# A loop on TensorE for the score matmuls of a decode attention kernel: register-addressed operands behind an opening matmul of zeros

## The chip, the cores and the metric

The kernel runs on one core of a Trainium2 chip. Its metric is device time in microseconds (us); in a profiled run it is 1.8 us longer than the span from the first to the last instruction. In this kernel TensorE does the matrix products, DVE (VectorE) the elementwise work and the reductions. In the traces TensorE's register and branch instructions are recorded apart from its matmuls; what runs the first is called its sequencer here, what runs the second the array. SBUF is the memory that the loads of this kernel fill, PSUM the one to which its matmuls write their sums, in banks. Each run below was taken beside runs of the kernel before on the same chip.

## The reference, cut to what matters

A residual stream `x` of one token (640 values) passes four attention layers in turn, A, B, A, B, each with its own key and value caches of 32 heads x 8192 positions x 192 values in bf16.

```python
q = (x @ wq).reshape(B, Sq, H, Dh)...                       # 1 token, 32 heads, 192
scores = jnp.einsum("bhqd,bhkd->bhqk", q, k_cache) * (Dh ** -0.5)
p = _softmax(scores, axis=-1)
o = jnp.einsum("bhqk,bhkd->bhqd", p, v_cache)
return o... @ wo
...
x = x + _A_ref(_layernorm(x), A_k_cache, A_v_cache, A_wq, A_wo)   # then B, A, B
```

Each cache element is used once in a layer, so nearly all the work is to bring 848 MB into the core and to touch it once.

## The kernel before

It works on pairs of heads. A pair's keys and values are 6144 KB each and go into eight slots of SBUF. A pair has two units `u`, one for each half of the positions. For a unit, DVE multiplies the keys by the query in four chunks of 48 of the 192 values, and TensorE adds the products up: 24 matmuls with the identity as the stationary operand sum 192 values down to eight, in one PSUM bank. A DVE reduction adds the last eight. The first matmul of a unit has `start=True`, the others `start=False`: the kernel relies on the first to overwrite what the bank held, and on the others to add to it. This is called opening the bank.

```python
def products(p, u):
    ...
    for c in range(4):                                       # DVE, four chunks
        d0 = c * QD
        e = DV.op(lambda v, d0=d0: v.tensor_tensor(
            k3[:, :, d0:d0 + QD], kin[:, :, d0:d0 + QD],
            q_sb[qi][:, d0:d0 + QD].unsqueeze(1).broadcast_to([P, JU, QD]), ALU.mult))
        chunks.append(e)
    S = SP_[u]
    PE.wait(last["S"][u], ev_const)
    for c in range(4):                                       # TensorE, six matmuls a chunk
        PE.wait(chunks[c])
        for r in range(QD // R):
            d0 = c * QD + r * R
            fin = c == 3 and r == QD // R - 1
            e = PE.op(lambda t, d0=d0, fin=fin: (
                t.matmul(S[:, :], lhsT=ident[:], rhs=k3[:, :, d0:d0 + R], start=True, stop=fin) if d0 == 0 else
                matmul_held(t, S[:, :], ident[:], k3[:, :, d0:d0 + R], False, fin)), signal=fin, bank=Su[u])
    freed[nt] = ev_S[p, u] = e                               # the key slot is free again

def softmax(p):
    ...
    for u in range(2):                                       # the reduction that waits for S
        ev_s = last["S"][u] = DV.op(lambda v, u=u: v.tensor_reduce(s[:, ...], SP_[u][:]..., AX.X, ALU.add), ev_S[p, u], ...)
```

`matmul_held` reuses the weights that are loaded: the trace of before has 128 weight loads for the 3072 score matmuls. After the softmax come the value matmuls and a gather, then the next pair's products. Loads are issued from SyncE as soon as the slot is free:

```python
def ahead():
    while issued[0] < len(plan):
        m = plan[issued[0]]
        if any(b not in freed for b in before[m]):
            return
        issued[0] += 1
        landed[m] = transfer(m)
```

Of the kernel before, what the change touches and what calls it, by code (L numbers as in the profile page):

```python
# [11 lines left out]
class Queue:  # L12
# [18 lines left out]
    def op(self, fn, *events, sem=None, inc=1, signal=True, bank=()):  # L31
# [11 lines left out]
            d[self] = (sem, self.counts[id(sem)])  # L43
        return sem, self.counts[id(sem)]

    def emit(self, eng):
        for it in self.items:
            if len(it) == 2:
                eng.wait_ge(*it)
            else:  # L50
                ins = it[0](eng)
                if it[1] is not None:
                    ins.then_inc(it[1], it[2])


def matmul_held(t, out, lhsT, rhs, start, stop, size=128, column=0):

    return t.add_instruction(mybir.InstMatmult(  # L58
        name=t.bass.get_next_instruction_name(), engine=mybir.EngineType.PE,
        ins=[t.lower_ap(rhs), t.lower_ap(lhsT, for_matmul_weights=True)], outs=[t.lower_ap(out)],  # L60
        start_tensor_calc=start, stop_tensor_calc=stop, tile_size=(128, size), tile_position=(0, column), ldweights=False))


PAIRS_W = 5
# [4 lines left out]
def build(nc, A_x, A_k, A_v, A_wq, A_wo, B_x, B_k, B_v, B_wq, B_wo, out):  # L69
    _, H, SK, DH = A_k.shape  # L70
    D = A_x.shape[-1]
    P = 128
# [6 lines left out]
    QD = DH // 4  # L79
    R = 512 // JU  # L80
# [17 lines left out]
    with ExitStack() as ctx:  # L98
        def sb(name, shape, dt):
            return ctx.enter_context(nc.sbuf_tensor(name, shape, dt))  # L100
# [4 lines left out]
        def sem(name):  # L105
            return ctx.enter_context(nc.semaphore(name))

        ident = sb("ident", [P, P], BF16)
# [38 lines left out]
        zero = sb("zero", [P, 33], BF16)  # L147
# [12 lines left out]
        Su = [(use["S0"],), (use["S1"],)]  # L160
# [6 lines left out]
        PE = Queue(sem("pPE"))  # L167
# [7 lines left out]
        e = PO.op(lambda g: g.memset(ident[:], 0.0))  # L175
# [6 lines left out]
        e = PO.op(lambda g: g.memset(mask, 0.0))  # L182
        for t in range(G):
            e = PO.op(lambda g, t=t: g.affine_select(
                out=mask, in_=mask, compare_op=ALU.not_equal, fill=1.0,
                base=-32 * t, pattern=[[-1, 2], [-2, VK]], channel_multiplier=1), e)
# [13 lines left out]
        def first_load(kind, l, p):  # L200

            n = (kind, pair(l, p))
            if l >= 2 and n in KEPT[l - 2]:
                return (l - 2, ORDER[l - 2]["pairs"].index(n[1]))
            return (l, p)

        def stays(kind, l, p):
            return l < 2 and (kind, pair(l, p)) in KEPT[l]
# [17 lines left out]
        for l in range(NL):  # L226
# [8 lines left out]
            for p in range(NPAIR):  # L235
# [17 lines left out]
                if p < NPAIR - 2:  # L253
                    if first_load("v", l, p) == (l, p):
                        plan += [("v", l, p, u) for u in range(2)]
                        if l == 2 and p == 1:
                            i = plan.index(("k", l, 1, 0))
# [135 lines left out]
        def need(n):  # L393

            while n not in landed:
# [3 lines that stand above are left out]
            return landed[n]  # L399
# [22 lines left out]
        def busy(n):  # L422

            PE.wait(ev_const, last["S"][0])
            for i in range(n):
                PE.op(lambda t, i=i: (
                    t.matmul(SP_[0][:, :], lhsT=ident[:], rhs=ident[:].unsqueeze(1).broadcast_to([P, 4, P]), start=True, stop=True)
                    if i == 0 else
                    matmul_held(t, SP_[0][:, :], ident[:], ident[:].unsqueeze(1).broadcast_to([P, 4, P]), True, True)),
                    signal=False, bank=Su[0])  # L430
# [14 lines left out]
        def layer(l, ev_z, ev_true):  # L445
# [7 lines left out]
            if l == 2:  # L453
                busy(2)
            e = DV.op(lambda v: v.scalar_tensor_tensor(out=nv[:], in0=mv[:, 0:1], scalar=mv[:, 0:1], in1=mv[:, 1:2],
                                                       op0=ALU.mult, op1=ALU.subtract))
            e = DV.op(lambda v: v.tensor_scalar(vs[:], nv[:], -float(DH), float(DH) * EPS, ALU.mult, ALU.add), e, last["rs"])
# [6 lines left out]
            if l < 2:  # L464
                e = need(("wq", l, 0))
# [4 lines left out]
            else:  # L470
                e = ev_first[l - 2]
                q_first = wq0[l - 2]
            PE.wait(e)
            for c in range(DC):
                for h in range(2):
                    e = PE.op(lambda t, c=c, h=h: t.matmul(
                        QM[64 * h:64 * h + 64, 0:DH], lhsT=xb[:, c:c + 1].broadcast_to([P, 64]),
                        rhs=q_first[:, c, h * DH:(h + 1) * DH], start=(c == 0), stop=(c == DC - 1)),
                        signal=(c == DC - 1 and h == 1), bank=QMu)
# [8 lines left out]
            def q_rows(g, r0=0, r1=None):  # L488

                n = ("wq", l, g)  # L490
                c0, k = Q_PARTS[g]
                t3 = wq_rows(l, g)[:, :, ORDER[l]["q1"] * PD if l < 2 else 0:]
                PE.wait(need(("wq", l, 0)) if l < 2 else need(n), ev_xb, last["O"], last["YB"], ev_first.get(l))
                r1 = k if r1 is None else r1
                for c in range(r0, r1):
                    for b in range(4):
                        w = min(512, QR - b * 512)
                        for r in range(3):
                            fin = c0 + c == DC - 1
                            o, x, y = (OY[32 * r:32 * r + 1, b * 512:b * 512 + w], xb[:, c0 + c:c0 + c + 1],  # L500
                                       t3[:, c, r * QR + b * 512:r * QR + b * 512 + w])
                            e = PE.op(lambda t, b=b, c=c, r=r, o=o, x=x, y=y, fin=fin: (
                                t.matmul(o, lhsT=x, rhs=y, start=c0 + c == 0, stop=fin) if b == 0 else
                                matmul_held(t, o, x, y, c0 + c == 0, fin, 32, 32 * r)),
                                signal=(c == r1 - 1 and b == 3 and r == 2), bank=OYu)
                freed.setdefault(n, e)
                if c0 + k == DC:
                    last["xb"] = e
                    last["rows"] = AC.op(
                        lambda a: a.activation(rows[0:65, :], OY[0:65, 0:QR], ACT.Copy, scale=rs[0:65, 0:1]),  # L510
                        e, ev_rs, last["qbc"], bank=OYu)
# [73 lines left out]
            def products(p, u):  # L585
                nk = ("k",) + first_load("k", l, p) + (u,)
                nt = ("t", l, p, u) if stays("k", l, p) else nk
                kin = slot[place[nk]].rearrange("p (j d) -> p j d", d=DH)
                k3 = slot[place[nt]].rearrange("p (j d) -> p j d", d=DH)
                qi = (l * NPAIR + p) % 2  # L590
                DV.wait(need(nk), need(nt), ev_q[p])
                chunks = []
                for c in range(4):
# [5 lines that stand above are left out]
                last["q"][qi] = chunks[-1]  # L599
                S = SP_[u]  # L600
                PE.wait(last["S"][u], ev_const)
                for c in range(4):
                    PE.wait(chunks[c])
                    for r in range(QD // R):
                        d0 = c * QD + r * R
                        fin = c == 3 and r == QD // R - 1
                        e = PE.op(lambda t, d0=d0, fin=fin: (
                            t.matmul(S[:, :], lhsT=ident[:], rhs=k3[:, :, d0:d0 + R], start=True, stop=fin) if d0 == 0 else  # L608
                            matmul_held(t, S[:, :], ident[:], k3[:, :, d0:d0 + R], False, fin)), signal=fin, bank=Su[u])
                freed[nt] = ev_S[p, u] = e  # L610

            def softmax(p):
# [107 lines left out]
            for n in [n for n in steps if n[1] == l]:  # L720
                if n[0] == "m":
                    products(*n[2:])
                elif n[0] == "s":
                    softmax(n[2])
# [37 lines left out]
            e = DV.op(lambda v: v.tensor_tensor(x_true[:], x_true[:], YB[:, 0:DC], ALU.add), ev_y, ev_true, bank=YBu)  # L762
# [5 lines left out]
        e = SP.op(lambda s: s.dma_start(out[0, 0].rearrange("(h n) -> h n", h=2), ev_z[0:33:32, :]), *ev_true, sem=semOUT, inc=16)  # L768
# [54 lines left out]
```

## Time and profile before

The first three runs had a median of 1985.24 us (1982.8 to 1987.34).

| What | Before | How to read it |
|---|---|---|
| Data queue's share of the 16 DMA engines | 99.6% | the resource that is hardly ever idle |
| TensorE, DVE busy | 65%, 61% | not free time: they run one after the other inside a pair |
| DVE's wait for keys | 133.3 + 97.2 us | 3.6 us in each of 64 pairs, what compute has to spare |
| DVE's reduction waits for S | 68.0 us | 1.06 us a pair, where a slower score stage shows first |

Its lines stand in the prediction below.

### The profile page before, as it was taken

The page shows a single profiled execution, that of the slowest core. Times are in us where ns is not written, and L with a number is a line of the kernel's source. Part 1 is how long each engine was busy: PE and PEld are TensorE (multiplying, and loading weights), DVE is VectorE, ACT ScalarE, POOL GpSimd, SP SyncE. Part 2 cuts the span into 40 slices and gives each one's busy share as a digit, 9 for nine tenths or more (in the row PEclk, how much of TensorE's full clock was granted, in tenths as well). Part 3 has the DMA queues.
Part 4 walks back from the last instruction along what each step waited for, and adds up shares of the span by engine and source line. Part 5 has one row for each costly group of instructions (what it writes and reads, how often), then busy time and mean ns, then how long its engine had stood idle before and what let it go on. Part 6 is the DMA issues. An engine that isn't in the chain of part 4 may idle for free.

```text
span 1980.6 us, 13926 instructions
## 1 busy us (share of the span) xinstructions
PE 1282.8 (65%) x8335; PEld 148.6 (8%) x3249; DVE 1201.2 (61%) x1377; ACT 139.6 (7%) x462; POOL 4.5 (0%) x23
## 2 busy tenths in 40 slices
PE   3567476566466666666785675666676766667658
PEld 0001001000100100100020010010002001001001
DVE  3566466467166656566745565665764765665756
ACT  0000000000000000000010000000000100000000
POOL 0000000000000000000000000000000000000000
PEclk9787777778687777777887777877886877777778
DMA  9999999999999999999999999999999999999998
GB/s 413 437 432 430 430 430 432 436 430 428 435 431 431 430 435 433 428 433 433 427 408 432 427 430 431 430 430 431 431 431 428 436 429 434 432 432 431 431 434 364
DMA packets 26786, 849.25 MB, mean 429 GB/s; under 512 B 3042, under 2 KB 3044, under 8 KB 3812
## 3 DMA queue, kind: packets, MB, share of 16 engines
q1 hardware_dynamic: 26580, 848.38, 99.6%
q8 instruction: 45, 0.74, 0.2%
q14 instruction: 17, 0.14, 0.0%
q10 hardware_dynamic: 144, 0.00, 0.0%
HBM read 848.36 MB, written 0.00 MB: 428 GB/s over the span
## 4 chain that ended last, share of the span: by engine, by line
DMA 67%; PE 17%; DVE 15%; ACT 1%; issue 0%; SPq 0%
DMA pool<-in_B_k_cache_dram 27%; DMA pool<-in_A_v_cache_dram 22%; DMA pool<-in_A_k_cache_dram 13%; DVE pool L595 13%; PE S L58 7%; DMA pool<-in_B_v_cache_dram 6%; PE OY L58 5%; PE OY L674 3%; DVE acc L693 1%; ACT p_sb L632 1%; DVE s_sb L617 1%; PE OY L535 1%; PE S L608 0%; DVE m_bf L619 0%; PE QM L622 0%
## 5 line engine op out<-in xcount | busy, mean ns | idle before, releaser
L595 DVE TENSOR_TENSOR pool<-pool,q_sb 128x3072 bf16<-128x3072 bf16 x512 | 860.8, 1751 | 231.9 <-DMA pool<-in_B_k_cache_dram 133.3
L58 PE MATMUL S<-pool,ident 128*128 128x512 bf16 x2944 | 788.6, 425 | 20.4 <-DVE pool L595 18.8
L704 PE MATMUL TB<-acc,small 128*1 128x192 f32 x240 | 82.7, 495 | 212.0 <-DVE acc L693 212.0
L58 PE MATMUL OY<-pool,p_sb 128*16 128x512 bf16 x1920 | 198.8, 490 | 0.0
L608 PE MATMUL S<-pool,ident 128*128 128x512 bf16 x128 | 62.4, 488 | 207.7 <-DVE pool L595 207.6
L692 DVE TENSOR_SCALAR acc<-OY,small 128x192 f32<-128x192 f32 x64 | 26.7, 418 | 277.9 <-PE OY L58 248.0
L674 PE MATMUL OY<-pool,p_sb 128*16 128x512 bf16 (+1 forms) x1216 | 145.9, 488 | 64.3 <-DMA pool<-in_A_v_cache_dram 59.7
L693 DVE SCALAR_TENSOR_TENSOR acc<-OY,small,acc 128x192 f32<-128x192 f32 x424 | 177.0, 418 | 14.9
L617 DVE TENSOR_REDUCE s_sb<-S 128x64 f32<-128x512 f32 x128 | 87.8, 686 | 68.0 <-PE S L58 68.0
L524 ACT ACTIVATE q_sb<-QM 128x192 bf16<-128x192 f32 x60 | 19.8, 330 | 952.4 <-PE QM L518 952.4
L715 ACT ACTIVATE rows<-TB,small 1x192 bf16<-1x192 f32 x120 | 43.1, 405 | 587.7 <-PE TB L704 587.7
L688 DVE RECIPROCAL small<-TB 1x2 f32<-1x2 f32 x64 | 11.2, 175 | 94.7 <-PE TB L647 75.3
L632 ACT ACTIVATE p_sb<-s_sb,small 64x128 bf16<-64x128 f32 x128 | 55.7, 435 | 160.9 <-DVE small L626 160.1
L608 PEld LDWEIGHTS S<-pool,ident 128*128 128x128 bf16 x128 | 12.9, 101 | 682.9 <-DVE pool L595 619.9
L647 PE MATMUL TB<-small,ones 128*1 128x2 f32 x120 | 11.4, 165 | 74.1 <-ACT p_sb L632 74.1
L674 PEld LDWEIGHTS OY<-pool,p_sb 128*16 128x16 bf16 (+1 forms) x1216 | 38.9, 105 | 207.4 <-issue 133.1
L622 PE MATMUL QM<-ident,m_bf 128*64 128x64 bf16 x128 | 14.1, 217 | 54.4 <-DVE m_bf L619 53.8
L704 PEld LDWEIGHTS TB<-acc,small 128*1 128x1 f32 x240 | 19.8, 102 | 311.2 <-DVE acc L693 284.0
L535 PE MATMUL OY<-oT,pool 128*128 128x1 bf16 x825 | 34.9, 178 | 2.5 <-ACT oT L580 2.5
L626 DVE TENSOR_REDUCE small<-QM 128x1 f32<-128x64 f32 x64 | 14.3, 224 | 35.2 <-PE QM L622 35.2
L535 PEld LDWEIGHTS OY<-oT,pool 128*128 128x128 bf16 x825 | 33.9, 131 | 4.5 <-ACT oT L580 3.2
L518 PEld LDWEIGHTS QM<-rows,one_b 1*64 1x64 bf16 x120 | 6.2, 100 | 347.1 <-issue 341.2
(75 smaller groups left out, 205.0 us busy)
## 6 DMA issues: line engine op xcount, KB each, us to landing
pool<-in_B_k_cache_dram SPq DMA_DIRECT2D x28, 6144.0 KB, 38.1
pool<-in_B_v_cache_dram SPq DMA_DIRECT2D x28, 6144.0 KB, 33.5
pool<-in_A_v_cache_dram SPq DMA_DIRECT2D x27, 6144.0 KB, 27.6
pool<-in_A_k_cache_dram SPq DMA_DIRECT2D x34, 3072.0 KB, 19.9
pool<-in_A_k_cache_dram SPq DMA_DIRECT2D x14, 6144.0 KB, 36.5
pool<-in_A_v_cache_dram SPq DMA_DIRECT2D x10, 3072.0 KB, 14.3
pool<-in_B_k_cache_dram SPq DMA_DIRECT2D x8, 3072.0 KB, 22.4
pool<-in_A_wo_dram SPq DMA_DIRECT2D x6, 2400.0 KB, 22.1
```

Of the source, the lines that this page charges most:

```text
L58: return t.add_instruction(mybir.InstMatmult(name=t.bass.get_next_instruction_name(), engine=mybir.EngineType.PE, ins=[t.lower_ap(rhs), t. ...
L524: lambda a: a.activation(q_sb[i][:], QM[:, 0:DH], ACT.Copy), e, last["q"][i], bank=QMu)
L535: e = PE.op(lambda t, i=i, c=c, f=y_first[0], fin=n[0] == "wol" and i == k - 1: t.matmul(YB[:, c:c + 1], lhsT=t3[:, i, c:D:DC], rhs=o[:, i ...
L595: e = DV.op(lambda v, d0=d0: v.tensor_tensor(k3[:, :, d0:d0 + QD], kin[:, :, d0:d0 + QD], q_sb[qi][:, d0:d0 + QD].unsqueeze(1).broadcast_t ...
L608: t.matmul(S[:, :], lhsT=ident[:], rhs=k3[:, :, d0:d0 + R], start=True, stop=fin) if d0 == 0 else
L617: lambda v, u=u: v.tensor_reduce(s[:, u * JU:(u + 1) * JU], SP_[u][:].rearrange("p (j r) -> p j r", r=R), AX.X, ALU.add), ev_S[p, u], last ...
L632: ev_p[p] = AC.op(lambda a, h=h, r=r: a.activation(p_sb[par][r, :, h], s[r, :], ACT.Exp, bias=negm[par][r, 0:1], accum_out=l_col[par][r, h ...
L674: t.matmul(o, lhsT=x, rhs=y, start=f, stop=fin) if c == 0 else
L692: v.tensor_scalar(acc[:], O[:, 0:DH], pick[:, 0:1], None, ALU.mult) if i == 0 else
L693: v.scalar_tensor_tensor(out=acc[:], in0=O[:, i * DH:(i + 1) * DH], scalar=pick[:, i:i + 1], in1=acc[:], op0=ALU.mult, op1=ALU.add)), e if ...
L704: e = PE.op(lambda t, h=h: t.matmul(TB[96:97, C_O + h * DH:C_O + (h + 1) * DH], lhsT=half[:, h:h + 1], rhs=acc[:], start=True, stop=True), ...
L715: last["TO"] = last["row_written"] = AC.op(lambda a, h=h: a.activation(orow[:, o0 + h * DH:o0 + (h + 1) * DH], TB[96:97, C_O + h * DH:C_O ...
```

## The change

The intent is a shorter instruction stream. The 24 unrolled matmuls become a loop of four passes on TensorE. A matmul must not open the bank in every pass, so a matmul of zeros opens it ahead of the loop.

```diff
+    def loop(self, event, n, fn, bank=()):
+        ...
+        def run(eng):
+            with eng.Fori(first, first + n) as i:
+                eng.wait_ge(sem, i)
+                fn(eng, i - first).then_inc(self.sem, 1)
...
                 PE.wait(last["S"][u], ev_const)
-                for c in range(4):
-                    PE.wait(chunks[c])
+                PE.op(lambda t: t.matmul(S[:, :], lhsT=ident[:], rhs=zero[:, 0:1].broadcast_to([P, 512]), start=True, stop=True), signal=False, bank=Su[u])
+
+                def chunk(t, c):
                     for r in range(QD // R):
-                        d0 = c * QD + r * R
-                        fin = c == 3 and r == QD // R - 1
-                        e = PE.op(lambda t, d0=d0, fin=fin: (
-                            t.matmul(S[:, :], lhsT=ident[:], rhs=k3[:, :, d0:d0 + R], start=True, stop=fin) if d0 == 0 else
-                            matmul_held(t, S[:, :], ident[:], k3[:, :, d0:d0 + R], False, fin)), signal=fin, bank=Su[u])
+                        e = matmul_held(t, S[:, :], ident[:], k3[:, :, bass.ds(c * QD + r * R, R)], False, True, bass_skip_group_check=True)
+                    return e
+
+                assert chunks[3][1] == chunks[0][1] + 3
+                e = PE.loop(chunks[0], 4, chunk, bank=Su[u])
```

More of the change, by code (lines that the diff above doesn't have):

```diff
@@ L44, in op @@
         return sem, self.counts[id(sem)]
+    def loop(self, event, n, fn, bank=()):
+        for d in bank:
+            self.wait(*[ev for q, ev in d.items() if q is not self])
+        sem, first = event
+        self.waited[id(sem)] = max(self.waited.get(id(sem), 0), first + n - 1)
+        self.counts[id(self.sem)] = self.counts.get(id(self.sem), 0) + n
+        def run(eng):
+            with eng.Fori(first, first + n) as i:
+                eng.wait_ge(sem, i)
+                fn(eng, i - first).then_inc(self.sem, 1)
+        self.items.append((run, None, 0))
+        for d in bank:
+            d[self] = (self.sem, self.counts[id(self.sem)])
+        return self.sem, self.counts[id(self.sem)]
     def emit(self, eng):
@@ L53, in emit, with matmul_held @@
                     ins.then_inc(it[1], it[2])
-def matmul_held(t, out, lhsT, rhs, start, stop, size=128, column=0):
+def matmul_held(t, out, lhsT, rhs, start, stop, size=128, column=0, **more):
     return t.add_instruction(mybir.InstMatmult(
@@ L60, in matmul_held @@
         ins=[t.lower_ap(rhs), t.lower_ap(lhsT, for_matmul_weights=True)], outs=[t.lower_ap(out)],
-        start_tensor_calc=start, stop_tensor_calc=stop, tile_size=(128, size), tile_position=(0, column), ldweights=False))
+        start_tensor_calc=start, stop_tensor_calc=stop, tile_size=(128, size), tile_position=(0, column), ldweights=False,
+        **more))
 PAIRS_W = 5
```

## The prediction

> **What bounds the kernel now.** I read the profile page first, from its busy shares to its DMA queues. The lines that matter:
>
> ```profile
> PE 1282.8 (65%) x8335; PEld 148.6 (8%) x3249; DVE 1201.2 (61%) x1377; ACT 139.6 (7%) x462; POOL 4.5 (0%) x23
> ...
> DMA  9999999999999999999999999999999999999998
> GB/s 413 437 432 430 430 430 432 436 430 428 435 431 431 430 435 433 428 433 433 427 408 432 427 430 431 430 430 431 431 431 428 436 429 434 432 432 431 431 434 364
> ...
> q1 hardware_dynamic: 26580, 848.38, 99.6%
> q8 instruction: 45, 0.74, 0.2%
> ...
> L595 DVE TENSOR_TENSOR pool<-pool,q_sb 128x3072 bf16<-128x3072 bf16 x512 | 860.8, 1751 | 231.9 <-DMA pool<-in_B_k_cache_dram 133.3
> L58 PE MATMUL S<-pool,ident 128*128 128x512 bf16 x2944 | 788.6, 425 | 20.4 <-DVE pool L595 18.8
> ...
> pool<-in_B_k_cache_dram SPq DMA_DIRECT2D x28, 6144.0 KB, 38.1
> pool<-in_A_k_cache_dram SPq DMA_DIRECT2D x34, 3072.0 KB, 19.9
> pool<-in_A_v_cache_dram SPq DMA_DIRECT2D x10, 3072.0 KB, 14.3
> ```
>
> No compute engine is above 65%, but the data queue fills 99.6% of the sixteen DMA engines' span, at 428 to 437 GB/s in nearly every slice. The kernel is the time to stream 848.38 MB: at 431 GB/s that is 1968 us, and the rest is a few us at the start and the end.
>
> The last three lines say how far ahead the stream is. 6144 KB take 14.6 us at 431 GB/s, yet from issue to landing the median is 38.1 us, so a key load typically finds 23.5 us of older transfers before it. For the 3072 KB value loads of the third layer it is only 14.3 against 7.3, so 7 us. I compared each issue with the landing of the load before it, through the whole trace: the next load is always issued before the last has landed. The smallest lead is 3.1 us, early in the third layer; about 8 us or more is usual elsewhere. A slot given back one or two microseconds later costs nothing.
>
> Next the waits of DVE, then one pair of heads in the timeline:
>
> ```profile
> DVE pool L595 <- DMA pool<-in_B_k_cache_dram: 133.3, 31, 13.4
> ...
> DVE pool L595 <- DMA pool<-in_A_k_cache_dram: 97.2, 27, 9.8
> ...
> DVE s_sb L617 <- PE S L58: 68.0, 64, 3.5
> ```
>
> ```profile
> 628.79 13.44 DVE L595 TENSOR_TENSOR pool<-pool,q_sb 128x3072 bf16<-128x3072 bf16 x8 [5.34 <-DMA pool<-in_B_k_cache_dram]
> ...
> 644.07 0.69 DVE L617 TENSOR_REDUCE s_sb<-S 128x64 f32<-128x512 f32 x1 [1.24 <-PE S L58]
> ...
> 657.87 3.43 DVE L595 TENSOR_TENSOR pool<-pool,q_sb 128x3072 bf16<-128x3072 bf16 x2 [3.08 <-DMA pool<-in_B_k_cache_dram]
> ```
>
> The pair takes 29.08 us, which is what 12.58 MB of keys and values take at 431 GB/s (29.2 us). Inside it the compute is a serial loop: eight products, score matmuls, softmax, value matmuls, gather, next products. So 65% busy does not mean a third of the time is free. What is free is DVE's wait for keys: 133.3 + 97.2 us over 64 pairs, 3.6 us a pair. That is the number the change has to fit into.
>
> [...]
>
> ```profile
> 1018.20 6.77 DVE pool L595 x4
> ...
> 1025.01 1.46 PE S L58 x6
> ```
>
> ```profile
> 1173.86 3.16 PE OY L535 x75
> ```
>
> Four products take 6.77 us, 1.69 each; the six matmuls of the last one end 1.46 us later, which fits starts about 0.21 us apart and a last matmul of 0.38. 75 weight loads with their matmuls in 3.16 us are 42 ns a pair. [...] 0.74 MB in 45 packets is 16.4 KB each.
>
> **The change, part by part.** The built program was compared engine by engine; DVE, ACT and SP keep their number of instructions.
>
> Removed: the unrolled copies, 24 matmuls for each of 128 units. In their place stand six matmuls in a loop of four passes. TensorE's stored stream goes from 11,237 instructions to 10,469, about 50 KB less to fetch. At 431 GB/s that is 0.1 us: nothing.
>
> Added first: 128 matmuls of zeros, 0.22 to 0.43 us each by the spacing above and its double in a cold stretch, about 27 to 55 us of busy time. They need only a free bank, so they run while TensorE waits for the first product. Path: about 0.
>
> Added second: sequencer work in each of 512 passes. The program has a register copy, six fused register operations (the first also waits for DVE's semaphore against a register), the six matmuls with their operand address in a register, an add and a compare-and-branch: 15 instructions where there were six. No duration of a fused operation is in this trace. [...] The array needs 6 x 0.216 = 1.3 and DVE delivers a chunk every 1.69. [...] only the last chunk's end moves, from 1.46 us after the product to about 1.8. Three of four waits already existed as semaphore waits.
>
> Sum: DVE's wait for the scores (68.0 us in 64 pairs, 1.06 each) becomes about 1.4 to 1.6, some 20 to 35 us in all, inside the 3.6 us a pair that DVE waits for keys anyway. On the path that sets the end there remain the layer starts and the tail. In the tail, the last pairs run without a wait for keys, and TensorE waits only this long for the last values:
>
> ```profile
> 1973.92 0.82 PE L674 MATMUL OY<-pool,p_sb 128*4 128x384 bf16 x16 [0.54 <-DMA pool<-in_B_v_cache_dram]
> ```
>
> Two pairs times 0.4 us, less 0.54, leaves under 1 us. The layer 3 start, with its lead of 3 to 5 us, may lose another one. Expected: 1985.2 + 1 to 3, so 1988 us.
>
> **Rivals.** (1) The sequencer becomes TensorE's bound. If P passes 1.69 us the lag grows by 8 x (P - 1.69) a pair. The first 3.6 us are hidden; a 2% loss (0.6 us a pair) needs about 4.2 [...], so P near 2.2 [...]. [...] For it: each matmul has its own register operation before it, and nothing here times one. [...] (2) Instruction fetch stalls. By their places in the program, 10 of the 128 loops straddle a 256-instruction boundary. [...] (3) A faster kernel, by fewer instruction fetches. The queue is 0.2% of the DMA time and loses a fifteenth of that; below 1980 us it cannot explain anything.
>
> **Range and chances.** Three quarters of my belief is in the hidden case, 1984 to 1992 us. A pass of 1.8 to 2.1 us, which costs only layer starts and tail (5 to 15 us), widens the upper end to 2003. The lower end, 1983, is the run-to-run spread of before. Rivals 1 and 2 together get 0.10, and lie outside the range. Faster by 2% [...]: 0.01. Within 2%: 0.89.
>
> **What would show it.** Right: data queue again above 99%; score matmuls still about 0.21 us apart when warm; wait of the s_sb reduction for S about 85 to 105 us; DVE's wait for keys smaller by about the same 20 to 40 us; instruction packets near 42. The step on sequencer cost is wrong if the six matmuls of a pass stand over 0.3 us apart, or the gap between passes exceeds 0.5 us. The prediction falls if DVE's wait for keys nearly vanishes, and the DMA share drops below 98%, or if TensorE stops for microseconds inside a loop with no product missing.

Where a cut is marked in the prediction, statements on the hardware that no trace or run of this case shows were taken out. Among them are terms of its sum: the author's estimates of c, the sequencer's time for one matmul with its register operation, and of what a pass boundary adds, and P, the time of a pass, worked out from them. The sum came to 1985.2 + 1 to 3, so 1988 us. Its step from 1.46 to about 1.8 us, and with it the 20 to 35 us of waits and the 0.4 us a pair, rested on the terms. In rival (1) P near 2.2 can be followed: 1.69 + 4.2 / 8.

Warm means a granted clock at full speed, cold one at half. In the traces of before and of the changed kernel the matmuls of a pass are 0.216 us apart (the median) where the granted clock is full (2013 and 2054 spacings) and 0.427 where it is half (496 and 451).

## The result, and the profile after

| | Before | Changed |
|---|---|---|
| Median of 6 runs | 1983.33 us | 1983.50 us |
| Range | 1982.80 to 1987.34 | 1982.92 to 1984.95 |
| Ratio | | 0.9997 (0.9984 to 1.001) |

A ratio is the mean time of one kernel's runs over that of the other's of the same rounds, so it is not quite the ratio of the medians. The time is the same. The forecast of 1 to 3 us more did not come.

From the page of the changed kernel, whose columns are those of the page before:

```profile
PE 1291.3 (65%) x8403; PEld 149.1 (8%) x3249; DVE 1201.6 (61%) x1377; ACT 139.8 (7%) x462; POOL 4.5 (0%) x23
...
q1 hardware_dynamic: 26580, 848.38, 99.5%
q8 instruction: 42, 0.69, 0.1%
...
L614 DVE TENSOR_TENSOR pool<-pool,q_sb 128x3072 bf16<-128x3072 bf16 x512 | 861.0, 1753 | 219.4 <-DMA pool<-in_B_k_cache_dram 125.6
L76 PE MATMUL S<-pool,ident 128*128 x3072 | 815.7, 423 | 223.5 <-DVE pool L614 220.7
```

The data queue is as full as before, the instruction packets went from 45 to 42 (0.74 to 0.69 MB), and TensorE is 8.5 us busier of 1983; the trace holds only 68 of the 128 matmuls of zeros, so this is a lower bound. The profiled run was the slowest of its six (1984.95 us); nothing is read from its total. Its waits, DVE's alone:

```profile
DVE pool L614 <- DMA pool<-in_B_k_cache_dram: 125.6, 30, 13.4
DVE pool L614 <- DMA pool<-in_A_k_cache_dram: 92.4, 27, 9.8
DVE s_sb L637 <- PE S L76: 79.3, 64, 4.3
```

The wait for S grew by 11.3 us, from 68.0 to 79.3. The wait for keys fell by 12.5 us, from 230.5 to 218.0. The kernel pays 0.18 us a pair in the score stage and takes it out of the time in which it would have waited for keys. The timeline shows the same pair as the prediction did:

```profile
628.80 13.44 DVE L614 TENSOR_TENSOR pool<-pool,q_sb 128x3072 bf16<-128x3072 bf16 x8 [5.41 <-DMA pool<-in_B_k_cache_dram]
...
642.40 1.46 PE L76 MATMUL S<-pool,ident 128*128 x6 [0.21 <-DVE pool L614]
...
643.89 0.69 DVE L637 TENSOR_REDUCE s_sb<-S 128x64 f32<-128x512 f32 x1 [1.05 <-PE S L76]
...
657.88 3.43 DVE L614 TENSOR_TENSOR pool<-pool,q_sb 128x3072 bf16<-128x3072 bf16 x2 [3.24 <-DMA pool<-in_B_k_cache_dram]
```

The pair again takes 29.08 us. The six matmuls of a pass still take 1.46 us, so the register operations do not spread them. They start 0.16 us after the product ends (628.80 + 13.44 = 642.24). Over all waits in the trace the median start after a product went from 0.053 to 0.158 us, and the end of a pair's second unit from 1.51 to 1.61 us after its last product. So a pass of the loop that waits for its product wakes 0.105 us later. Passes that don't wait follow each other as closely as before: at the 116 pass boundaries where the next product had been done for over 0.7 us, the median spacing of the matmuls is 0.216 us, as inside a pass and as in the kernel before.

### The profile page after: what moved, and what is told of

The parts are those of the page before. It is cut to its first block, busy times and chain, and to the rows that moved or that the text cites. A ratio compares the mean times of both kernels' runs of the same rounds, so it can differ in the third digit from the quotient of the medians.

```text
span 1983.2 us, 18730 instructions
## 1 busy us (share of the span) xinstructions
PE 1291.3 (65%) x8403; PEld 149.1 (8%) x3249; DVE 1201.6 (61%) x1377; ACT 139.8 (7%) x462; POOL 4.5 (0%) x23
## 3 DMA queue, kind: packets, MB, share of 16 engines
q1 hardware_dynamic: 26580, 848.38, 99.5%
## 4 chain that ended last, share of the span: by engine, by line
DMA 65%; PE 20%; DVE 12%; ACT 1%; issue 1%; SPq 0%
DMA pool<-in_B_k_cache_dram 27%; DMA pool<-in_A_v_cache_dram 20%; DMA pool<-in_A_k_cache_dram 14%; PE S L76 11%; DVE pool L614 10%; PE OY L76 4%; DMA pool<-in_B_v_cache_dram 4%; PE OY L694 3%; DVE acc L713 1%; ACT p_sb L652 1%; DVE s_sb L637 1%; PE OY L554 0%; DVE m_bf L639 0%; PE QM L642 0%; DVE small L646 0%
## 5 line engine op out<-in xcount | busy, mean ns | idle before, releaser
L76 PE MATMUL S<-pool,ident 128*128 x3072 | 815.7, 423 | 223.5 <-DVE pool L614 220.7
L712 DVE TENSOR_SCALAR acc<-OY,small 128x192 f32<-128x192 f32 x64 | 26.7, 418 | 280.5 <-PE OY L76 250.1
L637 DVE TENSOR_REDUCE s_sb<-S 128x64 f32<-128x512 f32 x128 | 88.1, 688 | 79.3 <-PE S L76 79.3
L621 PEld LDWEIGHTS S<-zero,ident 128*128 128x128 bf16 x128 | 12.9, 101 | 665.4 <-issue 665.2
L621 PE MATMUL S<-zero,ident 128*128 128x512 bf16 x68 | 25.8, 380 | 0.0
```

What stands on the lines that cost most here:

```text
L76: return t.add_instruction(mybir.InstMatmult(name=t.bass.get_next_instruction_name(), engine=mybir.EngineType.PE, ins=[t.lower_ap(rhs), t. ...
L621: PE.op(lambda t: t.matmul(S[:, :], lhsT=ident[:], rhs=zero[:, 0:1].broadcast_to([P, 512]), start=True, stop=True), signal=False, bank=Su[u])
L637: lambda v, u=u: v.tensor_reduce(s[:, u * JU:(u + 1) * JU], SP_[u][:].rearrange("p (j r) -> p j r", r=R), AX.X, ALU.add), ev_S[p, u], last ...
L712: v.tensor_scalar(acc[:], O[:, 0:DH], pick[:, 0:1], None, ALU.mult) if i == 0 else
```

## The experiments

Theory: the data stream sets the time, and the loop's cost of about 0.1 us a wake lies under DVE's wait for keys. Rival one: the loop costs a few microseconds on the path and something else, the zeros or the shorter program, pays them back. Rival two: the places where the prediction put the loss, tail and layer start, are hidden by the stream altogether. A third question is how near the sequencer came to being the bound.

### Each part alone: zeros_only and loop_only

```diff
 zeros_only, against the kernel before
+                PE.op(lambda t: t.matmul(S[:, :], lhsT=ident[:], rhs=zero[:, 0:1].broadcast_to([P, 512]), start=True, stop=False), ...)
                 for c in range(4):
                     ...                                      # unrolled, all 24 with start=False
 loop_only, against the changed kernel
-                PE.op(lambda t: t.matmul(... rhs=zero[:, 0:1].broadcast_to([P, 512]), start=True ...))
+                PE.wait(chunks[0])                           # six unrolled matmuls, the first opens the bank
+                ...
-                e = PE.loop(chunks[0], 4, chunk, bank=Su[u])
+                e = PE.loop(chunks[1], 3, chunk, bank=Su[u])
```

> Only the opening matmul of zeros, the 24 score matmuls of a unit stay unrolled. Stream theory (the DMA stream sets the time, the change's costs lie under DVE's wait for keys): ratio to before 1.000, within 0.1%; the first score matmul of a unit starts 0.05 us after its product, as before. Rival (the loop costs a few us on the path and something else pays them back, such as the zeros warming TensorE early): this run alone should be faster than before by 1 to 3 us, with a smaller wait of the s_sb reduction than the 68.0 us of before.

> The loop without the zeros: chunk 0 is unrolled and opens the bank itself, a loop of three passes does the rest. Stream theory: ratio 1.000 within 0.1%, wait of the s_sb reduction again 75 to 85 us (0.1 us more a pair than before). Rival (zeros pay the loop back): 1 to 3 us slower than before.

Measured: zeros_only 1983.86 us, loop_only 1983.57, before 1983.38; both ratios 1.0001 (0.9987 to 1.0015). The reduction's wait for S, from the waits of zeros_only and then of loop_only:

```profile
DVE s_sb L617 <- PE S L58: 72.8, 64, 3.7
```

```profile
DVE s_sb L641 <- PE S L76: 75.6, 64, 3.2
```

Neither part is clearly faster or slower than before. The zeros give nothing back: their run's wait for S is 72.8 us, above the 68.0 of before, and the mean granted clock of its profiled run is 0.784 against 0.782, so no warming by them shows. The two growths, 4.8 us for the zeros and 7.6 for the loop, add up to about the 11.3 of the changed kernel. In loop_only the unrolled first chunk starts 0.058 us after its product, while the median start after a wait is 0.158. The late wake belongs to the loop. Rival one has no support here, although the intervals leave -2.6 to +3.0 us open, so that the times alone don't exclude its 1 to 3 us.

### What a register-addressed matmul costs: narrow_loop and narrow_flat

```diff
 narrow_loop, against the changed kernel (wrong result on purpose)
+                PE.wait(chunks[3])
-                        e = matmul_held(t, S[:, :], ident[:], k3[:, :, bass.ds(c * QD + r * R, R)], ...)
+                        e = matmul_held(t, S[:, 0:64], ident[:], k3[:, 0:8, bass.ds(c * QD + r * R, R)], ...)
```

narrow_flat does the same to zeros_only.

> Sequencer cost by itself (wrong result on purpose): the looped matmuls are cut to 64 columns, [...] and TensorE waits for a unit's last product before the loop, so no pass waits for DVE. The spacing of matmuls in a pass is then c. [...] Since the whole kernel showed the spacing of 0.216 us unharmed, c has to be under 0.22. [...]

> The same 64-column matmuls unrolled, after an opening matmul of zeros and a wait for the last product (wrong result on purpose): the spacing without registers, 0.025 to 0.06 us, and no longer gap between chunks. It is the base for c of narrow_loop.

The timelines of TensorE, narrow_loop first:

```profile
648.97 0.77 PE L76 MATMUL S<-pool,ident 128*128 x6 [0.36 <-issue]
650.11 0.73 PE L76 MATMUL S<-pool,ident 128*128 x6 [0.37 <-issue]
651.21 0.77 PE L76 MATMUL S<-pool,ident 128*128 x6 [0.37 <-issue]
```

```profile
642.19 1.44 PE L58 MATMUL S<-pool,ident 128*128 128x64 bf16 x24 [4.81 <-DVE pool L595]
```

With nothing to wait for, a pass starts every 1.10 to 1.14 us. Inside it the median spacing is 0.104 us, over 2560 of them; from the last matmul of a pass to the first of the next it is 0.58 us, over 384, and none of these is above 0.79. The unrolled form has a spacing of 0.053 us. So c is 0.104 us, and a boundary adds 0.48 us. The author's estimates were too high for c and too low for the boundary. The sequencer's pass of 5 x 0.104 + 0.58 = 1.10 us lies under the array's 6 x 0.216 = 1.30 and DVE's 1.69. The sequencer runs ahead of the array during a pass, so the boundary is not seen in the full-width kernel, as its 0.216 us across boundaries showed above. The times are one look each: narrow_loop took 2012.16 us, beside 1983.65 for before. Making TensorE wait for the whole unit put its 4.4 us behind the last product. Where the added time appears was not split; the page has the stream slower in the slices of two layer starts and of the end (387, 373 and 264 GB/s against 434, 404 and 353 in the changed kernel). narrow_flat, with 1.44 us behind the last product, took 1983.23. The comparison with the reference passed for both, so it doesn't notice a wrong attention term in this problem, and does not vouch for the loop either.

### How much there is to spare: pass_plus2, pass_plus4, pass_plus8

```diff
                         e = matmul_held(t, S[:, :], ident[:], k3[:, :, bass.ds(c * QD + r * R, R)], ...)
+                    for r in range(4):                       # 2, 4 or 8
+                        e = matmul_held(t, S[:, :], ident[:], zero[:, 0:1].broadcast_to([P, 512]), False, True, ...)
                     return e
```

> The changed kernel with 2 more matmuls of zeros in each pass. A warm pass takes 8 x 0.216 = 1.73 us, just above DVE's 1.69; the lag at the end of a unit grows by 0.45 to 0.8 us a pair. Stream theory: time unchanged within 0.3% (1982 to 1990), DVE's wait for keys falls from 218 us by about 30 to 60. If nothing were hidden: 64 x 0.5 = +30 us or more.

> The changed kernel with 4 more matmuls of zeros in each pass: 10 x 0.216 = 2.16 us a pass, 8 x 0.47 + 0.9 = 4.7 us more a pair. The break-even of the prediction was a pass of about 2.2 us, so this stands on the edge: +0.2 to +3% (1987 to 2045), wait for keys under 80 us. Time clearly the same with keys still waited for over 150 us would put the break-even higher than the prediction had it.

> The changed kernel with 8 more matmuls of zeros at the end of each pass (result unchanged). A pass on a warm TensorE takes 14 x 0.216 = 3.0 us against DVE's 1.69, so the lag grows by 8 x 1.33 = 10.7 us a pair; with 3.4 us of waits for keys and about 1 us of waits for values to hide in: (10.7 - 4.4) x 64 = +400 us, 2330 to 2450 us, and the wait for keys nearly gone. If the slack were a third of the span, as the 65% busy suggests (10 us a pair): +50 us.

| | Median, us | Ratio to before | Over before, us | Wait for S, us | Wait for keys, us |
|---|---|---|---|---|---|
| changed kernel | 1983.50 | 0.9997 | 0.2 | 79.3 | 218.0 |
| 2 more | 1992.46 | 1.0043 (1.0026 to 1.006) | 8.8 | 273.7 | 112.8 |
| 4 more | 2119.84 | 1.0686 (1.0662 to 1.0709) | 136.2 | 482.9 | 40.6 |
| 8 more | 2564.31 | 1.2927 (1.2908 to 1.2946) | 580.7 | 935.3 | 37.4 |

The data queue and the two waits of pass_plus4, from its page and its waits:

```profile
q1 hardware_dynamic: 26580, 848.38, 94.1%
```

```profile
DVE s_sb L639 <- PE S L76: 482.9, 71, 9.6
DVE pool L614 <- DMA pool<-in_B_k_cache_dram: 22.5, 4, 13.4
DVE pool L614 <- DMA pool<-in_A_k_cache_dram: 18.1, 8, 9.8
```

The same in pass_plus8:

```profile
q1 hardware_dynamic: 26580, 848.38, 79.0%
```

Against the changed kernel the wait for S grew by 194.4, 403.6 and 856.0 us, and the time by 9.0, 136.3 and 580.8. The hidden part is the difference: 185, 267 and 275 us. It saturates at about 270 us, which is 4.2 us a pair. After that every microsecond is paid. In the two larger runs the waits for keys cover 177 to 181 of it. Most of the rest is DVE's wait for the value matmuls, which fell from 250.1 us to 183.0, 179.4 and 167.9.

All three estimates missed. For 2 more I expected at most 1990 us and a wait for keys smaller by 30 to 60; it was 1992.46 and 105.2. The two larger came out far above their ranges. I had taken a warm TensorE, with matmuls 0.216 us apart, for every pass. In these traces it comes cold to a pair: in the first pass of a pair 84 to 91% of the spacings are the slow ones of about 0.427 us, and in pass_plus8 such a pass took 4.6 us on the mean against 3.03 for the later ones. Over a whole run the mean granted clock is higher with more added matmuls: 0.787 in the changed kernel, then 0.831, 0.877 and 0.895. In the changed kernel a warm pass of 1.30 us catches up with DVE's 1.69 afterwards. With 2 more, a pass of 1.73 us no longer does: the matmuls of a pair's second unit end 4.42 us after its last product on the mean, against 1.80. So the wait for S grew by 3.0 us a pair, not 0.45 to 0.8, and in pass_plus8 by 13.4, not 10.7.

### What the loop costs where compute sets the time: half_flat, half_zeros, half_loop

```diff
-                    f = lambda s: s.dma_start(pool[:, i * TS:(i + 2) * TS], r)
+                    k = TS if {i, i + 1} <= filled else 2 * TS     # a slot's first load is whole
+                    filled.update((i, i + 1))
+                    f = lambda s: s.dma_start(pool[:, i * TS:i * TS + k], r[:, 0:k])
```

The loads of single units are halved in the same way. The three are the kernel before, the zeros alone and the changed kernel. Each slot's first load stays whole, so 470.89 MB are moved and not half of 848. Their results are wrong; the comparison passed here too.

> The kernel before, but each key or value load after a slot's first one moves only half its bytes (wrong result on purpose), so that the stream no longer sets the time. Stream theory: far faster, about 1650 to 1750 us (pair loop 29.1 us less the 3.6 us of waits for keys, 64 times, plus layer starts); DMA share near 60%; DVE's wait for keys near zero. If something other than the stream set the time of before, it stays above 1900.

> The same halved loads with the opening zeros and unrolled score matmuls. Zeros run while TensorE has nothing else: within 2 us of half_flat. If the zeros warm TensorE usefully: faster than half_flat by over 3 us.

> The changed kernel with the same halved loads: what the loop costs where the compute loop sets the time. From the traces of the whole kernels (score matmuls wake 0.158 us after the product against 0.053, unit ends 1.61 after its last product against 1.51): +0.10 to 0.17 us a pair, +7 to +11 us over half_flat, 0.4 to 0.6%. By the prediction's own estimate (0.3 to 0.4 us a pair, plus layer starts): +20 to +28 us. If the loop is free in truth: within 2 us.

| | Median, us | Range | Ratio to before |
|---|---|---|---|
| half_flat | 1682.98 | 1680.27 to 1686.35 | 0.8479 (0.8468 to 0.849) |
| half_zeros | 1685.45 | 1682.10 to 1696.75 | 0.8507 (0.8484 to 0.8529) |
| half_loop | 1703.47 | 1695.71 to 1710.77 | 0.8591 (0.8569 to 0.8614) |

The queue of half_flat is no longer full, though it is above the 60% expected:

```profile
q1 hardware_dynamic: 26580, 470.89, 69.3%
```

Fewer bytes alone take 300 us away, so the stream does set the time of the whole kernel. half_zeros lies 2.5 us above half_flat, where within 2 was expected; their intervals overlap. The loop costs 20.5 us here, more than the 7 to 11 I expected from the late wake. It lies in the 20 to 28 us that the prediction's delay would have given, but by luck, as the following shows. DVE's waits, half_flat first, then half_loop:

```profile
DVE acc L697 <- PE OY L58: 152.7, 55, 4.1
DVE s_sb L622 <- PE S L58: 96.4, 71, 4.5
```

```profile
DVE acc L717 <- PE OY L76: 163.5, 56, 4.1
DVE s_sb L642 <- PE S L76: 103.3, 70, 4.7
```

The wait for S grew by 6.9 us, as the late wake has it. The other 10.8 us are waits for the value matmuls (`OY`), which the change does not touch. From pair to pair the period is either about 24 or about 25.5 us. The short pairs have a median of 23.954 us in half_flat and 24.057 in half_loop, which is the late wake again. Pairs of 25.2 to 25.9 us were 5 in half_flat, 7 in half_zeros and 14 in half_loop. Two rows of half_loop's timeline, one from a short pair and one from a long one, show what differs:

```profile
133.46 0.63 PE L76 MATMUL OY<-pool,p_sb 128*16 128x512 bf16 x8
...
238.52 1.09 PE L76 MATMUL OY<-pool,p_sb 128*16 128x512 bf16 x8
```

In the long pair the value matmuls run at half the rate. It is so in all pairs of these two kinds: in every short pair of the three traces the spacings between value matmuls add up to 2.42 us, in every long one to 3.5 to 4.1. Of 63 periods, 49 in each trace are of the two kinds. From half_flat to half_loop these 49 grew by 17.7 us, which is about 49 x 0.10 for the late wake and 9 x 1.45 for nine more long pairs; the other 14 became 1.5 us shorter. Together this is 16.1 of the 16.2 us by which the spans of the two traces differ. The medians differ by 20.5; half_loop is spread over 15 us, and one run of half_zeros (1696.75) lies inside its range.

Why does a period 0.1 us longer meet the slow clock more often? The traces show a granted clock that changes on a grid of 3413 ns, called windows here: in half_flat and half_loop all granted-clock records last a whole number of 3413 ns, and in the traces of before and of the changed kernel all 206 and 216 records, each of full or of half clock, start a whole number of 3413.3 ns after the first. Seven windows are 23.89 us, so, as an estimate from this length and the medians above, a pair of 23.95 drifts by 0.06 us against them and one of 24.06 by 0.17. The traces have this too: from one short pair to the next, the first value matmul starts 0.06 us later in its window in half_flat and 0.16 in half_loop. In the 147 pairs of the two kinds in the three traces, the pair is long whenever this start is over 2.1 or under 0.6 us into a window, and short whenever it is between 0.68 and 2.08, without exception. A larger drift leaves the good stretch sooner. This ties the long pairs to the window. It does not fix their number, which also hangs on where in the window a row of pairs begins: half_zeros, with the drift of half_flat, has 7. No run here varied the period by itself.

### Whether the tail and a layer start are on the path: tail_6us and start_6us

```diff
 tail_6us: before the last value matmuls of the last layer
-                            busy(6)
+                            busy(34)
 start_6us: in the third layer's start, before its query matmuls
-                busy(2)
+                busy(30)
```

> The changed kernel with 28 more filler matmuls on TensorE just before the last value matmuls of the last layer, 28 x 0.216 = 6.0 us. If the tail is on the path as the prediction had it, with 0.5 to 1.0 us of wait for the last values to hide in: +5.0 to +5.5 us over the changed kernel, about 1988.5. If the stream hides the tail too: +0 to 1 us. In the first case the prediction's tail step was right about the place and its delay of 0.4 us a pair was too large; in the second the place itself was wrong.

> The changed kernel with 28 more filler matmuls in the serial chain at the start of the third layer, 6.0 us warm and up to 8 to 9 us as TensorE comes in cold there. The least lead of the data stream there is 3.0 us. Stream theory: the first 3 us or so are hidden, so +3 to +6 us, and the lead in the trace falls to zero there. If the layer start had no lead (prediction's 'may lose another one' for delays of 1 us): +6 to +9 us. If later slack swallows it: 0.

Measured: tail_6us 1988.71 us (ratio 1.0029, 1.0015 to 1.0043), start_6us 1989.30 (1.0029, 1.0016 to 1.0043), before 1983.38. The tail's rows, from the timeline:

```profile
1973.06 7.29 PE L76 MATMUL S<-ident 128*128 128x512 bf16 x33
1980.28 0.82 PE L694 MATMUL OY<-pool,p_sb 128*4 128x384 bf16 x16
```

The last values had landed 5.4 us before the matmuls that read them began. The time grew by 5.2 us over the changed kernel (5.3 over the kernel before of the same rounds), where 6.0 us of work were added: the tail is on the path and hides less than 1 us. Rival two falls for the tail.

The layer start, first in the changed kernel, then in start_6us:

```profile
1018.24 13.44 DVE L614 TENSOR_TENSOR pool<-pool,q_sb 128x3072 bf16<-128x3072 bf16 x8 [1.41 <-ACT q_sb L504]
```

```profile
1025.23 13.44 DVE L614 TENSOR_TENSOR pool<-pool,q_sb 128x3072 bf16<-128x3072 bf16 x8 [8.25 <-ACT q_sb L504]
```

TensorE is cold there: the granted clock is 0.61 from 1003 to 1018 us of the changed kernel, and in start_6us 29 of the filler matmuls took 7.89 us. Products start 7.0 us later, and the kernel takes 5.8 us longer by the medians. Two loads were now issued after the load before them had landed, by 0.4 and 0.9 us, counted to the start of the issue. From there each took 2.28 us longer than its bytes at 431 GB/s (1.47 MB in 5.70 us, 3.15 MB in 9.58 us). So the stream stood still for 0.4 + 2.28 and 0.9 + 2.28, about 5.9 us in all, which is what the kernel lost. By these two loads an issue has to come about 2.3 us ahead. The smallest lead of the changed kernel, counted in the same way, is 3.39 us (3.04 from the end of the issue, as the prediction counted its 3.1), so about 1.1 us was to spare. It is a soft margin: around that load the sixteen DMA engines already stand idle for 0.3 us in the changed kernel and 0.2 in the kernel before. I had expected 3 us to be hidden. Rival two falls for the layer start as well. Against this 1.1 us the loop's own delay is small: the lead went from 3.49 to 3.39 us.

## Why the prediction was right or wrong

**The bound was right.** The page after again has a full data queue, and halved loads make the kernel 15% faster. The reading of the serial pair loop was right too: the prediction allowed 3.6 us of waits for keys a pair, and the runs with more work hide 2.9 us (2 more) to 4.3 (8 more) a pair.

**The forecast was wrong in one term of the sum.** The step that failed is "only the last chunk's end moves, from 1.46 us after the product to about 1.8", and with it "Two pairs times 0.4 us, less 0.54, leaves under 1 us. The layer 3 start ... may lose another one. Expected: 1985.2 + 1 to 3". The prediction does not derive the 0.34 us between 1.46 and 1.8; it is about the size of the author's estimate of the boundary, counted in series, which no trace had shown. Measured, the boundary is overlapped in a full-width pass, c is 0.104 us, and the last chunk's end moves by 0.10 us. Two pairs at that size are 0.2 us in the tail, under its 0.54 us of wait; at the layer start they are 0.1 us against 1.1. So both places can hide the real delay, and the path term is zero within what the runs resolve. The sum was also rounded up: its own terms, 2 x 0.4 - 0.54 in the tail and one microsecond at the layer start, make 1.3 us, where it says 1 to 3 and then takes nearly the upper end, 1988. And the microsecond at the layer start had no working behind it: even a delay of 0.4 us is under the 1.1 to spare. The places themselves were well chosen, as tail_6us and start_6us show: a delay of the size of those runs is paid there. The flat sentence "A slot given back one or two microseconds later costs nothing" is too strong for the third layer's start.

**The base was also high.** 1985.24 us was a median of three with one run at 1987.34. Six runs gave 1983.33, so a part of the gap between 1988 and 1983.5 was never the change's.

**The tests it named.** Data queue above 99%: right, 99.5%. Warm spacing of 0.21 us: right. About 42 instruction packets: right. Wait for S of 85 to 105 us: wrong, 79.3. Wait for keys smaller by 20 to 40 us: wrong, 12.5. Both were sized with the lag that failed above.

**The rivals.** The sequencer as the bound did not come. With the measured boundary, 5c + (c + 0.48) reaches the prediction's P of 2.2 us at c near 0.29, 2.8 times the measured one, so it was far off in c. But the break-even itself was put too high. A loss of 2% was expected near a P of 2.2 us; pass_plus4, with passes of 2.16 us, lost 6.9%, because 8 x (P - 1.69) leaves out the backlog of the cold first pass. Stalls of instruction fetch did not come either. The 10 loops that straddle a boundary are in the program of narrow_loop too, and no pass boundary there took over 0.79 us. The 256 instructions of rival (2) are one packet: the stream is 768 instructions and three packets of 16.4 KB shorter. Nothing was gained by it.

## What to carry to other kernels

Where a data stream sets the time, first find how much a stage may slow down per period before the stream notices; here about 3 to 4 us of 29, though the engines looked a third idle. A cost placed on a path still needs its size measured: a small kernel that starves the array shows a sequencer's cost directly, and would have put the measured 0.104 us in the place of a guess. A loop that is free under a full stream cost about 1% here once the stream was lighter (20.5 us of 1683), and over half of that (9 x 1.45 us) was the slow clock of matmuls that were never touched.
